# Deviations regrouped by two VectorE transposes and four small transfers instead of a TensorE product

## The chip, the cores and the metric

One core of one Trainium2 chip. The metric is the device time of one execution in microseconds; the median of several runs is quoted. Everything is float32. The engines of the core are TensorE (PE, with its weight loads PEld), VectorE (DVE), ScalarE (ACT), GpSimd (POOL) and SyncE (SP, which only issues transfers). Each runs its own instructions in order; semaphores hold one engine back for another, or for the landing of a transfer.

## The reference

Two blocks, one behind the other. The first mixes tokens by a filter in the frequency domain, the second is a feed-forward layer with a SoLU activation (h times its softmax) and a layer norm:

```python
batch, seq, dim = 8, 3136, 256            # 25088 tokens; d_ff = 1024
X = np.fft.rfft(x, axis=1)
Y = X * (filt_r + 1j * filt_i)[None]
t = np.fft.irfft(Y, n=3136, axis=1).reshape(25088, 256)

h = t @ w_in                               # 256 -> 1024
e = np.exp(h - h.max(-1, keepdims=True))
solu = h * e / (e.sum(-1, keepdims=True) + 1e-9)
mu = solu.mean(-1, keepdims=True)
var = ((solu - mu) ** 2).mean(-1, keepdims=True)
out = ((solu - mu) / np.sqrt(var + 1e-6) * g_ln) @ w_out   # 1024 -> 256
```

What the change touches is 1 / sqrt(var + ...), one number for each token ("deviation" in the code, `rs`). It scales the output rows of the last product.

## The kernel before

**Stages.** The first some 150 us convert the weights, transform batch element 0 and start element 1. From then on the feed-forward layer of the tokens that are ready runs together with the transforms of the later elements: element e's tokens are used while element e+1 is transformed. The last element's transform is over at about 1200 us; behind that only the feed-forward layer runs.

**Blocks, pairs, groups.** The 25088 tokens are 196 blocks of 128. Two blocks are a pair j (98 of them), because both products are done on pairs by a scheme with seven products of half size (`product(j, m)` at L759 and `project(p, m)` at L895, m = 1 to 7) and sums that GpSimd makes (`sum_of`, L738). Four blocks are a group g (49).

**Steps.** `step(k)` for k = 0 to 204 writes out by hand, for each engine, the order in which work of different blocks is interleaved: even and odd steps differ. A block passes `product`, `keep` (ScalarE copies a half of h from PSUM, L769), `finish` (VectorE makes another half and the row's maximum, L780 and L783), `exponential` (ScalarE, L793), `normalize` (VectorE, L805), `square` (ScalarE, the variance, L813), `turn` (VectorE transposes 32x32 blocks, L823), `regroup`, and some nine steps after its start `project`, `keep_out` (ScalarE, L911), `finish_out` (VectorE, L915) and `store_out` (SP, L923). No scheduler moves anything: each engine gets its instructions in the order in which the functions are called.

**Regrouping.** `project` needs solu with features on partitions. `turn` transposes only within 32x32 blocks, so `regroup` moves 32 partitions at a time by transfers from SP (L840, eight of 128 KB for a pair). The tokens then stand in another order: partition 32b + i of block a holds token 32a + i of block b of the group. The scale of an output row has to stand in the same order. That is what the changed part does, once for a group:

- `deviations(g)`, even step, GpSimd: variance plus floor (L850), power -1/2 (L851) into rs, 128 x 4 (partition: token in the block, column: block); then `wide` = rs times a table of zeros and ones, 128 x 4 x 32 (L853).
- `regroup_deviations(g)`, two steps later, behind `project(p, 4)`: one product on TensorE, `wide` as weights and four columns of the table (`turn_t`) as the moving side (L859, two passes), into four spare columns of a PSUM bank (`places`), and a copy by ScalarE into rs_t (L862).
- `keep_out` and `finish_out` take a column of rs_t as the scale.

**Queues.** SP issues the regroup transfers, the stores of the output, and in part of the steps the loads of x (L257); ScalarE and GpSimd issue the transforms' other loads and stores. All transfers that SP and ScalarE issue take eight completion semaphores in turn; a transfer is issued only when the last one on its semaphore has landed.

**PSUM.** `project(p, 2)` writes the bank that `finish_out(p - 1, 1, 0)` reads; `product(j, 4)` adds to a bank that `finish(j, k, 1)` reads. These are TensorE's two nearest waits for VectorE in an odd step.

Of the kernel before, what the change touches and what calls it, by code (L numbers as in the profile page):

```python
# [9 lines left out]
FP32 = mybir.dt.float32  # L10
I32 = mybir.dt.int32
AFT = mybir.ActivationFunctionType
ALU = mybir.AluOpType
# [4 lines left out]
P = 128  # L18
# [79 lines left out]
def kernel(  # L98
# [10 lines left out]
    nc = tc.nc  # L109
# [6 lines left out]
    there_dram = nc.inline_tensor(  # L116
        np.ascontiguousarray(de_host[:, :, 0].reshape(NP, P, P).transpose(1, 0, 2)), name="there_tbl").ap()
    one_dram = nc.inline_tensor(np.eye(P, dtype=np.float32), name="one_tbl").ap()
    rows = np.arange(P)[:, None]
    turn_dram = nc.inline_tensor(np.concatenate(  # L120
        [rows % 32 == np.arange(32), rows // 32 == np.arange(4)], 1).astype(np.float32),
        name="turn_tbl").ap()

    def pool(name, bufs, space=None, stack=ctx):
        kw = {} if space is None else {"space": space}
# [5 lines left out]
    small = pool("sm", 4)  # L131
# [15 lines left out]
    neg_half, floor_sb = small_consts[:, 0:4], small_consts[:, 4:5]  # L147
# [268 lines left out]
    with ExitStack() as st:  # L416
# [226 lines left out]
    def psum(name):  # L643
        return ps_t.tile([P, 2, C], FP32, name=name, tag="t")
# [13 lines left out]
             for name, bufs in (("r", 4), ("diff", 1), ("t2", 1), ("p", 1), ("g", 1))}  # L658
    pools["de"] = pool("de1", 2)
    spread = pool("spread", 1)  # L660
    turn_t = spread.tile([P, 36], FP32, name="turn_t", tag="turn_t")
    second.pools = pools
    for c, at, n, kind, dims in (
            (0, 0, 4 * C, "t2", "p (v c) -> p v c"), (0, 4 * C, 4 * C, "f", "p (v k c) -> p v k c"),
# [51 lines left out]
    def load_de(sp, u):  # L716
# [3 lines left out]
                            in_=de_dram[i:i + pairs].rearrange("i p k u q -> p i (k u q)"))  # L720
        return de

    turns, variances, solu_ts, solu_sums, spreads, rss, pos, ots, places, regrouped = (
        {} for _ in range(10))
    sums, ms, hs, nmaxs, es, esums, floors, solus, squares = ({} for _ in range(9))


# [120 lines left out]
    def deviations(g):  # L848
        rs = small.tile([P, 4], FP32, name=f"rs_{g}", tag="rs", bufs=2)
        nc.gpsimd.tensor_tensor(out=rs, in0=variances.pop(g), in1=floors.pop(g), op=ALU.add)  # L850
        nc.gpsimd.tensor_tensor(out=rs, in0=rs, in1=neg_half, op=ALU.pow)  # L851
        spreads[g] = wide = spread.tile([P, 4, 32], FP32, name=f"wide_{g}", tag="wide")
        nc.gpsimd.tensor_tensor(  # L853
            out=wide, in0=turn_t[:, 0:32].rearrange("p (o i) -> p o i", o=1).broadcast_to([P, 4, 32]),
            in1=rs.rearrange("p (b o) -> p b o", o=1).broadcast_to([P, 4, 32]), op=ALU.mult)

    def regroup_deviations(g, ps):

        nc.tensor.matmul(out=ps, lhsT=spreads.pop(g).rearrange("p b i -> p (b i)"), rhs=turn_t[:, 32:36],  # L859
                         start=True, stop=True)  # L860
        rss[g] = small.tile([P, 4], FP32, name=f"rs_t_{g}", tag="rs_t")
        nc.scalar.copy(out=rss[g], in_=ps)  # L862

    def project_sums(p, step):

# [14 lines left out]
    def project(p, m):  # L880

        alone = m == 3 and p in last
        bank = 2 if alone else {1: 0, 6: 0, 5: 0, 3: 0, 2: 1, 7: 1, 4: 1}[m]
        if alone:
            pos[p, bank] = ps_m.tile([P, DFF // 2], FP32, name=f"o{m}_{p}", tag="m0")[:, 0:P]
        elif m in (1, 2):
            ps = ps_o.tile([P, DFF // 2], FP32, name=f"o{m}_{p}", tag=f"o{bank}")
            pos[p, bank] = ps[:, 0:P]
            places[p] = ps[:, P:P + 4]
        s1, s2, s3, s4 = solu_sums[p]  # L890
        lhs = {1: solu_ts[p, 0][0], 2: solu_ts[p, 0][1], 4: solu_ts[p, 1][1], 5: s1, 6: s2, 7: s3,
               3: s4}[m]
        w = w_out_sb[:, {1: 0, 2: 1, 3: 2, 5: 3, 6: 4, 7: 5, 4: 6}[m]]
        for f in range(KF // 2):
            nc.tensor.matmul(out=pos[p, bank], lhsT=lhs[:, f, :], rhs=w[:, f, :],  # L895
                             start=f == 0 and (m in (1, 2, 7) or alone), stop=True,
                             skip_group_check=True)
# [104 lines left out]
    pairs = blocks // 2  # L1002

    def step(k):
        j, odd = divmod(k, 2)
        p = j - (LAG - 1) // 2 if odd else j - (LAG + 1) // 2
        if not 0 <= p < pairs:
            p = None
        hid, proj = k < blocks, p is not None
# [23 lines left out]
        if not odd:  # L1033
            if hid and k > LAG:
                product(j, 1)
                keep(j, k, 0)
            if 2 <= k < blocks:
                exponential(k - 2)
            if proj:
                project(p, 5)  # L1040
                keep_out(p, 1, (1, 1) if p in last else (0, 1))
            if p in last:
                keep_out(p, 0, (0, 1))
                finish_out(p, 1, 1, (1, 1), 1)
# [12 lines left out]
            if 3 <= k < blocks + 3:  # L1057
                square(k - 3)
            if hid:
                product(j, 6)  # L1060
                keep(j, k + 1, 0)
            if proj:
                project(p, 3)
                if p not in last:
                    keep_out(p, 0, (0, 1))
                project(p, 4)
            if j >= 4 and j % 2 == 0 and j - 4 < pairs:
                regroup_deviations((j - 4) // 2, places.pop(p) if proj else psum("ps_rs")[:, 0, 0:4])
            for job in spectrum_loads[k]:
                job()  # L1070
            if 0 <= j - 3 < pairs - 2:
                regroup(j - 3, 0)
                regroup(j - 3, 1)
            elif j - 3 == pairs - 2:
                regroup(j - 3, 1, nc.scalar.dma_start, range(2))
                regroup(j - 3, 0)
                regroup(j - 3, 1, parts=range(2, 4))
                regroup(j - 2, 0)
                regroup(j - 2, 1, parts=range(2))
            if 0 <= j - 4 < pairs:  # L1080
                project_sums(j - 4, 1)
            if j - 3 == pairs - 2:
                regroup(j - 2, 1, nc.gpsimd.dma_start, range(2, 4))
            if 0 <= j - 3 < pairs and j % 2:
                deviations((j - 3) // 2)
            if hid:
                product(j, 7)
            if p in last:
                finish_out(p, 0, 1, (0, 1), 2)
                finish_out(p, 1, 0, (1, 0), 1)  # L1090
                store_out(p)
            if 2 <= k < blocks + 2:
                normalize(k - 2)
            for job in second_parts[k] + middle[k] + first_parts[k]:
                job()
            if proj and p not in last:
                finish_out(p, 1, 0, (1, 0), 1)
                store_out(p)
        else:
            if hid and k >= LAG:  # L1100
                product(j, 5)
                keep(j, k - 1, 1)
                finish(j, k, 1, (k - 1, 1), 2)
            for job in early[k]:
                job()
            if proj:
                project(p, 1)
                keep_out(p, 0, (0, 0))
                project(p, 2)
                finish_out(p, 0, 0, (0, 0), 1)  # L1110
            if 2 <= k < blocks + 2:
                exponential(k - 2)
            if hid:
                product(j, 3)
                product(j, 4)
            if proj:
                project(p, 6)
                project(p, 7)
            for job in second_parts[k] + middle[k]:
                job()  # L1120
            if 3 <= k < blocks + 3:
                turn(k - 3)
            if hid:
                finish(j, k - 1, 1, None, 0)
                finish(j, k, 0, (k, 0), 2)
            if 2 <= k < blocks + 2:
                normalize(k - 2)
            if proj:
                keep_out(p, 1, (1, 0))
            if 3 <= k < blocks + 3:  # L1130
                square(k - 3)
            for job in first_parts[k]:
                job()
        if k == 0:
            for n in range(7):
                prepare_w_out(n)
# [2 lines left out]

    with tc.manual_schedule():  # L1140
        pair_sums(0)
        nc.gpsimd.dma_start(out=turn_t, in_=turn_dram)
        for load in first_loads:
            load()
        for k in range(blocks + LAG):
            step(k)
# [30 lines left out]
```

## Time and profile before

| | before |
|---|---|
| median of 3 runs | 1594.7 us (1591.9 to 1596.17) |
| the profiled execution: its time | 1601.33 us |
| its span, first to last instruction | 1599.6 us |
| mean granted TensorE clock | 0.994 |
| TensorE busy | 1551.8 us (97%) |
| VectorE busy | 1250.7 us (78%) |
| GpSimd busy | 1169.7 us (73%) |
| ScalarE busy | 921.4 us (58%) |
| bytes moved by DMA | 311.13 MB, mean 195 GB/s |

Busy time is that of instructions that work; register, semaphore and transfer-issuing instructions are not in it. Matmuls are pipelined, so the time from one start to the next, and not the duration of one, is what a matmul costs. SP has no work but to issue transfers; its entries carry a q, for its sequencer's queue.

### The profile page before, as it was taken

Reading aid. Unit: us, or ns where it says so; the run is one execution under the profiler, and the core shown is the slowest. Engines: PE = TensorE matmul, PEld = TensorE weight load, DVE = VectorE, ACT = ScalarE, POOL = GpSimd, SP = SyncE. Lnnn points to the kernel's source line nnn. Section 1 sums busy time; section 2 is a strip of 40 time slices with the busy share of each in tenths; the row PEclk is TensorE's granted clock in tenths of the full one; section 3 lists DMA queues with packets and bytes.
Section 4 is the critical chain, followed back from the end, with each engine's and each line's share of the span. In section 5 each row is a group of like instructions: output and inputs, shape, how many; then the busy total and the mean of one; then the engine's idle time right before and its main releaser. Section 6 shows DMA issues by size and latency. Waiting matters only on the chain.

```text
span 1599.6 us, 36769 instructions
## 1 busy us (share of the span) xinstructions
PE 1551.8 (97%) x12828; PEld 1058.8 (66%) x12828; DVE 1250.7 (78%) x2248; ACT 921.4 (58%) x1874; POOL 1169.7 (73%) x1371
## 2 busy tenths in 40 slices
PE   5998999999999999999999999999999999999997
PEld 1463566666666676677666677667766777777777
DVE  1887878897987788876988789887888777777673
ACT  2246555656665656666565655666565656666663
POOL 5546886789677868796779867797766766676765
PEclk8999999999999999999999999999999999999999
DMA  9989878786987589766886679766784444343434
GB/s 266 290 282 269 247 215 236 215 217 181 255 241 222 155 229 256 211 183 178 221 231 202 166 193 251 204 189 179 215 224 132 126 133 122 103 113 94 116 105 116
DMA packets 343802, 311.13 MB, mean 195 GB/s; under 512 B 27834, under 2 KB 310099, under 8 KB 343619
## 3 DMA queue, kind: packets, MB, share of 16 engines
q1 hardware_dynamic: 271476, 170.45, 40.6%
q0 software_dynamic: 33744, 98.81, 21.0%
q10 hardware_dynamic: 38400, 39.53, 8.2%
q8 instruction: 104, 1.70, 0.5%
q14 instruction: 78, 0.64, 0.1%
HBM read 124.51 MB, written 81.40 MB: 129 GB/s over the span
## 4 chain that ended last, share of the span: by engine, by line
PE 84%; DMA 9%; DVE 2%; POOL 1%; issue 1%; SPq 1%; ACT 0%; DVEq 0%; POOLq 0%; ACTq 0%
PE m L759 35%; PE o L895 34%; DMA solu_t<-turn 4%; PE py L386 4%; PE pc L313 3%; PE pb L313 3%; PE pa L281 2%; DMA x<-in_x_dram 2%; DMA f<-in_filt_r_dram 1%; SPq L840 1%; PE idler L563 1%; PE pa L238 1%; PE py L409 1%; DMA out_dram<-ot 1%; POOL u L738 1%
## 5 line engine op out<-in xcount | busy, mean ns | idle before, releaser
L895 PEld LDWEIGHTS o<-w_out_sb,solu_t 128*128 128x128 f32 x3136 | 381.5, 192 | 50.2 <-issue 43.6
L895 PE MATMUL o<-w_out_sb,solu_t 128*128 128x128 f32 x3136 | 400.9, 276 | 3.6 <-DVE ot L915 2.9
L759 PE MATMUL m<-w_in_sb,s 128*128 128x512 f32 x784 | 399.0, 610 | 2.7 <-ACT h L769 1.8
L895 PEld LDWEIGHTS o<-w_out_sb,u 128*128 128x128 f32 x2352 | 307.1, 192 | 138.9 <-issue 106.0
L895 PE MATMUL o<-w_out_sb,u 128*128 128x128 f32 x2352 | 310.6, 275 | 2.5 <-POOL u L738 1.8
L759 PE MATMUL m<-w_in_sb,y 128*128 128x512 f32 x588 | 307.6, 606 | 1.5 <-DVE h L780 1.1
L805 DVE SCALAR_TENSOR_TENSOR h<-e,h 128x1024 f32<-128x1024 f32 x196 | 304.1, 1551 | 0.1
L769 ACT COPY h<-m 128x512 f32<-128x512 f32 x294 | 173.2, 589 | 206.5 <-PE m L759 187.0
L911 ACT ACTIVATE ot<-o,rs_t 128x128 f32<-128x128 f32 x392 | 143.6, 368 | 245.2 <-PE o L895 243.8
L738 POOL TENSOR_TENSOR u<-solu_t 128x512 f32<-128x512 f32 x98 | 135.5, 1383 | 195.6 <-DMA solu_t<-turn 133.6
L783 DVE CUSTOM_DVE_ANT_0 h<-m,h 128x512 f32<-128x512 f32 x196 | 134.2, 685 | 176.8 <-ACT h L769 103.0
L813 ACT ACTIVATE h<-h,nmu 128x1024 f32<-128x1024 f32 x196 | 225.0, 1148 | 52.0 <-DVE turn L823 51.8
L823 DVE STREAM_TRANSPOSE turn<-h 128x1024 f32<-128x1024 f32 x196 | 243.1, 1240 | 3.2
L793 ACT ACTIVATE e<-h,nmax 128x1024 f32<-128x1024 f32 x196 | 225.4, 1150 | 7.9 <-DVE h L805 6.5
L738 POOL TENSOR_TENSOR u<-solu_t,u 128x512 f32<-128x512 f32 x98 | 137.7, 1405 | 95.8 <-PE o L895 95.5
L759 PEld LDWEIGHTS m<-w_in_sb,s 128*128 128x128 f32 x784 | 128.1, 191 | 89.5 <-issue 68.9
L915 DVE SCALAR_TENSOR_TENSOR ot<-o,rs_t,ot 128x128 f32<-128x128 f32 x299 | 103.7, 347 | 98.8 <-ACT ot L911 59.0
L738 POOL TENSOR_TENSOR u<-u,solu_t 128x512 f32<-128x512 f32 x98 | 159.1, 1624 | 15.5 <-PE o L895 6.4
L759 PEld LDWEIGHTS m<-w_in_sb,y 128*128 128x128 f32 x588 | 96.6, 191 | 96.7 <-issue 46.6
L738 POOL TENSOR_TENSOR solu_t<-solu_t,solu_t 128x512 f32<-128x512 f32 x98 | 153.9, 1571 | 0.9
L738 POOL TENSOR_TENSOR s<-y 128x128 f32<-128x128 f32 x196 | 99.8, 509 | 0.5
L386 PEld LDWEIGHTS py<-wb_t,t 50*64 50x64 f32 x3584 | 57.6, 134 | 42.9 <-issue 18.7
(126 smaller groups left out, 1969.1 us busy)
## 6 DMA issues: line engine op xcount, KB each, us to landing
solu_t<-turn SPq DMA_DIRECT2D x780, 128.0 KB
out_dram<-ot SPq DMA_DIRECT2D x196, 128.0 KB
t<-d POOLq DMA_DIRECT2D x112, 200.0 KB, 7.0
d<-x POOLq DMA_DIRECT2D x100, 200.0 KB, 5.3
f<-f_dram POOLq DMA_DIRECT2D x39, 512.0 KB, 8.1
t<-d ACTq DMA_DIRECT2D x37, 512.0 KB
d<-g POOLq DMA_DIRECT2D x36, 512.0 KB, 5.1
x<-in_x_dram SPq DMA_DIRECT2D x112, 98.0 KB
```

The costliest lines, as they stand in the source:

```text
L386: nc.tensor.matmul(out=views[g][64 * h:64 * h + 64, cb, i, :], lhsT=t4[rows, i, c0:c0 + 64], rhs=wb_t[rows, 0:N1], start=True, stop=True)
L738: nc.gpsimd.tensor_tensor(out=out, in0=in0, in1=in1, op=op)
L759: nc.tensor.matmul(out=ms[j, bank], lhsT=lhsT, rhs=w_in_sb[:, w, :], start=m in (1, 2, 7), stop=True, skip_group_check=True)
L769: nc.scalar.copy(out=h_half(k, i), in_=ms[j, 0])
L783: nc.vector.tensor_tensor_reduce(out=h_half(k, i), in0=ms[j, bank], in1=h_half(*kept), scale=1.0, scalar=sofar, op0=ALU.add, op1=ALU.min, ...
L793: nc.scalar.activation(out=e, in_=hs[k], func=AFT.Exp, bias=nmaxs.pop(k)[:, 1:2], scale=-1.0, accum_out=esums[g][:, i:i + 1])
L805: nc.vector.scalar_tensor_tensor(out=solu, in0=e, scalar=SHRINK, in1=solu, op0=ALU.mult, op1=ALU.mult, accum_out=nmu)
L813: nc.scalar.activation(out=solu, in_=solu, func=AFT.Square, bias=nmu, scale=-float(DFF), accum_out=variances[g][:, i:i + 1])
L823: nc.vector.transpose(out=turns[g][:, :, i, :], in_=solus[k].rearrange("p (f j) -> p f j", j=32))
L895: nc.tensor.matmul(out=pos[p, bank], lhsT=lhs[:, f, :], rhs=w[:, f, :], start=f == 0 and (m in (1, 2, 7) or alone), stop=True, skip_group_ ...
L911: nc.scalar.activation(out=out_half(p, *to)[0], in_=pos[p, 0], func=AFT.Copy, scale=rs)
L915: nc.vector.scalar_tensor_tensor(out=ot, in0=pos[p, bank], scalar=rs, in1=out_half(p, *kept)[0], op0=ALU.mult, op1=ALU.add)
```

## The change

`deviations` ends with the power -1/2, which is written into the first four columns of a cleared tile `lines` (128 x 32). A new function, called at the end of the odd step that follows, transposes `lines` on VectorE by 32x32 blocks and has SP move four times four rows of 32 numbers (512 bytes a transfer) to the partitions where a second transpose can pick them up. `regroup_deviations`, at its old place in the step, is now that second transpose, into an rs_t of 128 x 32 of which four columns are used. The table, `wide`, the product on TensorE, its place in PSUM and the copy by ScalarE are gone.

```diff
@@ pools
-    turn_t = spread.tile([P, 36], FP32, name="turn_t", tag="turn_t")
+    lines = small.tile([P, 32], FP32, name="lines", tag="lines", bufs=1)
+    turned_rs, crossed_rs = (spread.tile([P, 32], FP32, name=n, tag=n) for n in ("turned_rs", "crossed_rs"))
+    for cleared in (lines, crossed_rs):
+        nc.gpsimd.memset(cleared, 0.0)
@@ def deviations(g):
         nc.gpsimd.tensor_tensor(out=rs, in0=variances.pop(g), in1=floors.pop(g), op=ALU.add)
-        nc.gpsimd.tensor_tensor(out=rs, in0=rs, in1=neg_half, op=ALU.pow)
-        spreads[g] = wide = spread.tile([P, 4, 32], FP32, name=f"wide_{g}", tag="wide")
-        nc.gpsimd.tensor_tensor(
-            out=wide, in0=turn_t[:, 0:32].rearrange("p (o i) -> p o i", o=1).broadcast_to([P, 4, 32]),
-            in1=rs.rearrange("p (b o) -> p b o", o=1).broadcast_to([P, 4, 32]), op=ALU.mult)
-
-    def regroup_deviations(g, ps):
-
-        nc.tensor.matmul(out=ps, lhsT=spreads.pop(g).rearrange("p b i -> p (b i)"), rhs=turn_t[:, 32:36],
-                         start=True, stop=True)
-        rss[g] = small.tile([P, 4], FP32, name=f"rs_t_{g}", tag="rs_t")
-        nc.scalar.copy(out=rss[g], in_=ps)
+        nc.gpsimd.tensor_tensor(out=lines[:, 0:4], in0=rs, in1=neg_half, op=ALU.pow)
+
+    def cross_deviations(g):
+
+        nc.vector.transpose(out=turned_rs, in_=lines)
+        to = crossed_rs.rearrange("(b r) i -> r b i", r=32)
+        for a in range(4):
+            nc.sync.dma_start(out=to[a], in_=turned_rs[32 * a:32 * a + 4])
+
+    def regroup_deviations(g):
+        rss[g] = spread.tile([P, 32], FP32, name=f"rs_t_{g}", tag="rs_t", bufs=4)
+        nc.vector.transpose(out=rss[g], in_=crossed_rs)
@@ def step(k), even steps
             if j >= 4 and j % 2 == 0 and j - 4 < pairs:
-                regroup_deviations((j - 4) // 2, places.pop(p) if proj else psum("ps_rs")[:, 0, 0:4])
+                regroup_deviations((j - 4) // 2)
@@ def step(k), end of odd steps
             for job in first_parts[k]:
                 job()
+            if 0 <= j - 3 < pairs and j % 2:
+                cross_deviations((j - 3) // 2)
```

Also gone are the table in DRAM and its load (`nc.gpsimd.dma_start(out=turn_t, in_=turn_dram)`), and `places`.

More of the change, by code (lines that the diff above doesn't have):

```diff
@@ L118 @@
     one_dram = nc.inline_tensor(np.eye(P, dtype=np.float32), name="one_tbl").ap()
[L119 to L122, printed above, removed]
     def pool(name, bufs, space=None, stack=ctx):
@@ L721, in load_de @@
         return de
-    turns, variances, solu_ts, solu_sums, spreads, rss, pos, ots, places, regrouped = (
-        {} for _ in range(10))
+    turns, variances, solu_ts, solu_sums, rss, pos, ots, regrouped = (
+        {} for _ in range(8))
     sums, ms, hs, nmaxs, es, esums, floors, solus, squares = ({} for _ in range(9))
@@ L888, in project @@
             pos[p, bank] = ps[:, 0:P]
-            places[p] = ps[:, P:P + 4]
         s1, s2, s3, s4 = solu_sums[p]
@@ L1141 @@
         pair_sums(0)
-        nc.gpsimd.dma_start(out=turn_t, in_=turn_dram)
         for load in first_loads:
```

## The prediction

> **What bounds the kernel now.** I read the page first, then the busy time by stretch, the groups, SP's own waits, and last the timelines of one place where the change sits.
>
> ```profile
> span 1599.6 us, 36769 instructions
> PE 1551.8 (97%) x12828; PEld 1058.8 (66%) x12828; DVE 1250.7 (78%) x2248; ACT 921.4 (58%) x1874; POOL 1169.7 (73%) x1371
> PE 84%; DMA 9%; DVE 2%; POOL 1%; issue 1%; SPq 1%; ACT 0%; DVEq 0%; POOLq 0%; ACTq 0%
> ```
>
> TensorE is the bound: busy 97% of the span and 84% of the chain that ended last. So TensorE time taken away is gained in full, and every wait put in front of TensorE is lost in full. The stretches tell how much room the others have:
>
> ```profile
> 600.00:800.00 200.00, 199.99 (x1867) 138.59 (x1866) 165.09 (x299) 121.16 (x249) 157.53 (x187) 1.00 0.77 210
> 1400.00:1500.00 100.00, 100.00 (x578) 72.67 (x577) 73.82 (x139) 63.08 (x131) 70.74 (x77) 1.00 0.40 106
> ```
>
> The columns are busy us of TensorE, its weight loads, VectorE, ScalarE and GpSimd, then the clock and the DMA share. Until about 1200 us VectorE is busy 83% and the DMA engines 77%; after it 74% and 40%. TensorE leaves nothing unused in either.
>
> **What is removed.** Groups by form, with the mean ns of one after the busy time:
>
> ```profile
> L859 PE MATMUL o<-turn_t,wide 128*128 128x4 f32 x96 | 13.6, 212 | 0.0
> L862 ACT COPY rs_t<-o 128x4 f32<-128x4 f32 x48 | 7.8, 162 | 25.4 <-PE o L859 25.4
> L823 DVE STREAM_TRANSPOSE turn<-h 128x1024 f32<-128x1024 f32 x196 | 243.1, 1240 | 3.2
> ```
>
> Matmuls overlap, so 212 ns is not what one costs TensorE. In the timeline the first pass of L859 starts at 805.26 and the product behind it at 805.40. In every even step with L859 the last pass of project 4 is followed by product 7 after 0.254 us, in every one without it after 0.112 us. So one regrouping costs TensorE 0.142 us, and 49 cost 7.0 us. That is the gain. The 49 copies on ScalarE (8 us, and 25.4 us of waiting for L859) and the 49 multiplications on GpSimd (49 x 0.40 = 20 us) lie beside TensorE; I price them at nothing, because ScalarE is idle 42% and GpSimd 27%. Two clears of small tiles and one table load at the start change sides, beside the first 120 us.
>
> **What is added on VectorE.** 98 transposes of 128x32. The only transpose in the trace takes 1.240 us for 1024 columns; 32 of them would be 0.04 us, and the shortest VectorE row is 0.08 us. Between 0.04 and 0.35 (L915, 128x128) I take 0.1 us: 10 us of VectorE in all, small beside its idle 349 us. It enters below as 0.1 us on each side of the transfers.
>
> **What is added on SP, and the new wait.** In the order of the built program the first transpose of a group stands at the end of an odd step, behind normalize (L805). The four transfers follow in SP's queue, ahead of the next eight regroup transfers (L840). The second transpose stands in the middle of the next even step, right in front of the next L805, and waits for all four landings. VectorE runs in order, so L805, the spectrum's products, the joins, finish_out (L915) and the next step's finish (L783) queue behind that wait. Group 20 in the trace of before, VectorE:
>
> ```profile
> 799.31 0.08 DVE L805 DVE_READ_ACCUMULATOR h<-e,h 128x1 f32 x1
> 799.42 1.25 DVE L823 STREAM_TRANSPOSE turn<-h 128x1024 f32<-128x1024 f32 x1
> 800.72 0.69 DVE L783 CUSTOM_DVE_ANT_0 h<-m,h 128x512 f32<-128x512 f32 x1
> 802.05 0.35 DVE L915 SCALAR_TENSOR_TENSOR ot<-o,rs_t,ot 128x128 f32<-128x128 f32 x1 [0.63 <-ACT ot L911]
> 802.32 2.13 DVE L805 SCALAR_TENSOR_TENSOR h<-e,h 128x1024 f32<-128x1024 f32 x1
> ```
>
> The first transpose would start at 799.39, the second is due at 802.32: a window of 2.9 us. Over the groups it is 2.05 to 4.3 us (one 7.8). SP's timeline there, and two rows of its waits:
>
> ```profile
> 798.02 14.07 SPq L840 DMA_DIRECT2D solu_t<-turn  x8
> 799.68 1.79 SPq L840 DMA_DIRECT2D solu_t<-turn  x1
> 805.39 0.58 SPq L840 DMA_DIRECT2D solu_t<-turn  x1
> ```
>
> ```profile
> SPq L840 <- DMA out_dram<-ot: 46.6, 41, 3.9
> SPq L840 <- DMA solu_t<-turn: 19.6, 20, 2.5
> ```
>
> The transfers of SP and ScalarE use eight semaphores in turn, and each waits until the last holder of its semaphore has landed. The fourth regroup transfer here could only go at 805.39, because its semaphore belonged to a store of the output that SP issued at 793.68. In the changed order the four small transfers take exactly these places in the queue and in the turn. So the fourth goes at 805.4, not at 801.
>
> Price of one trip. Issue: L257 and L840 take 0.29 to 0.75 us on SP where they don't wait, with no order by size; I take 0.45, with 0.15 and 0.65 as ends. From the end of the issue to the landing: a regroup transfer between partitions on an empty queue takes 1.71 to 1.76 us (the fastest tenth), the quickest store 2.8 us; I take 1.74, since the new transfers also stay in SBUF. Another 0.2 us before and after for transpose and semaphore. With nothing in the way: 0.2 + 4 x 0.45 + 1.74 + 0.2 = 3.9 us, 1 us over the usual window. In group 20: 805.4 + 0.45 + 1.74 + 0.2 = 807.8, a VectorE stall of 5.5 us.
>
> The Trainium skill ("DMA: Bandwidth & Descriptors", section "Anatomy of one DMA — SWDGE (gpsimd) path") gives about 2.0 us as the fixed cost of any transfer, on a path other than SP's. By that figure the loss below would be 60 us and not 55.
>
> What the stall costs TensorE:
>
> ```profile
> 807.28 0.34 DVE L915 SCALAR_TENSOR_TENSOR ot<-o,rs_t,ot 128x128 f32<-128x128 f32 x1
> 807.20 1.95 PE L895 MATMUL o<-w_out_sb,solu_t 128*128 128x128 f32 x16
> ```
>
> The second eight of these 16 passes (project 2, from 808.09) write the bank that L915 frees at 807.62. The slack is 0.5 us, so TensorE would lose 5.0 us here. I read window, semaphore landings and slack (the smaller of project 2 behind L915 and product 4 behind L783, plus VectorE's idle time between) the same way at groups 0 to 47:
> - 21 groups before 1200 us with loads of x (L257) just ahead in SP's queue: stalls of 69.6 us, of which slack leaves 47.4.
> - 13 other groups of that stretch: 16.3 us of stall, 7.6 left.
> - 14 groups after it: 16.8 us of stall, slack 1.5 to 3.0 us, nothing left.
> - The last group: its transfers stand behind two output stores that SP issues at 1580.74 and 1581.44, so the second transpose ends near 1586 where the L915 behind it ran at 1578.43. TensorE then waits in project 2 of pair 96 from 1579.6, less what it waits there anyway for GpSimd until 1582.5: 5 us.
>
> Loss 55 + 5, gain 7: +53 us on the profiled execution of 1601.3 us, 3.3%. On the median of 1594.7 us that is 1647 us. The ends: with 0.15 us an issue the 55 is 44, with 0.65 it is 64, with stores' landings of 2.8 us 75; so +42 to +73, 1637 to 1668. Given back by less crowded queues at a slower pace: 0 to 20 us, taken as nothing.
>
> The regroup transfers behind the four: in loaded groups the first four go up to 8 us later, the other four (due at 6 to 8 us after the first transpose) 2 to 3 us later. GpSimd waits 133.6 us for them already (44 times) and TensorE waits behind these sums hardly at all, some 13 us; so I price this at nothing. If that cover fails, 2 us in each of 34 groups is 68 us.
>
> The Trainium skill ("VectorE: DVE Perf Modes", section "Rules for kernel authors") sends a 128x128 transpose to TensorE where PSUM will do, since VectorE's covers 32x32 blocks only. Here the row speaks on the same side from its price: 0.142 us of TensorE against a trip of 3.9 us.
>
> **The rivals.**
> 1. Forecast, 0.60: the trip outlasts the slack in the loaded groups; 1647, own range 1620 to 1675.
> 2. Faster, 0.17: the trip fits into window and slack everywhere. Its place is the 21 loaded groups; it decides where four transfers land within 3.9 us of the first transpose, that is, if the semaphores ahead are free in time. For it: windows plus slack are 4.7 to 6.1 us after 1200 us. Against it: SP's fourth regroup issue, 4 to 9 us after the first transpose's place in 12 of those groups. Then only the 7.0 us count: 1588.
> 3. No change, 0.07: loss and gain cancel, with 7 us of stall left over from the 55; 1590 to 1599.
> 4. Worse, 0.16: slack does not come back between groups, or regrouping becomes late. VectorE has 5 us idle in a group of 29 us, less than the stall of a loaded group; with all 104 us of stall before 1200 us at the dear issue counted, +102 us: 1697; with the 68 us of late regrouping 1715.
> That the change does not do what it says is out: the built order has 98 transposes, 196 such transfers and no L859.
>
> **How the numbers follow.** A measurement of this kernel tells about 0.3% from no change. Faster 0.17, same 0.07, slower 0.76. The range leaves out the lower half of case 2 and most of case 4 above 1690: 1588 to 1690.
>
> **What would show it.** Right: VectorE's wait in front of the second transpose is a large new row, released by the small transfers, some 85 us before 1200 us and 17 us after; TensorE's new idle time ends on L915; the stretch 1400 to 1500 does as much work as before. Wrong: a mean trip under 3 us; TensorE idle where no second transpose precedes; or GpSimd's wait for regrouped tokens grown and TensorE waiting behind it.

## The result, and the profile after

| | before | after |
|---|---|---|
| median of 6 runs each, same chip | 1595.4 us | 1652.2 us |
| ratio, 95% interval | | 1.0354 [1.0321, 1.0388] |
| the profiled execution: its time, its span | 1601.3, 1599.6 us | 1664.4, 1662.3 us |
| mean granted TensorE clock | 0.994 | 0.979 |

The changed kernel is 3.5% slower, some 57 us. Its profiled execution is the slowest of its six runs, so differences between the two traces (62.7 us of span) are a little larger than that between the medians.

The head of the page of the changed kernel:

```profile
span 1662.3 us, 36908 instructions
PE 1563.2 (94%) x12730; PEld 1062.2 (64%) x12730; DVE 1248.9 (75%) x2346; ACT 914.7 (55%) x1825; POOL 1145.6 (69%) x1323
```

98 passes fewer on TensorE, 98 instructions more on VectorE. TensorE's idle time has gone from 47.8 us (1599.6 - 1551.8) to 99.1 us, and its busy time has gone up by 11.4 us although it has less to do. Both need an answer. The stretches of the changed kernel, with columns as in the prediction:

```profile
600.00:800.00 200.00, 193.52 (x1745) 133.33 (x1745) 158.35 (x301) 116.29 (x235) 147.46 (x175) 0.99 0.74 202
1400.00:1500.00 100.00, 100.00 (x687) 72.40 (x687) 75.59 (x148) 62.34 (x125) 71.27 (x72) 1.00 0.40 106
```

While the transforms run, TensorE loses 6.5 us in 200; behind them it loses nothing. The waits, with engine, line, what is waited for, then us in total, times and the longest. First two rows of before, then those of the changed kernel, then SP's own wait in it:

```profile
POOL u L738 <- DMA solu_t<-turn: 133.6, 44, 8.2
PE o L895 <- DVE ot L915: 2.9, 4, 1.2
```

```profile
DVE rs_t L861 <- DMA crossed_rs<-turned_rs: 116.4, 48, 8.9
POOL u L737 <- DMA solu_t<-turn: 122.9, 42, 8.7
PE o L893 <- DVE ot L913: 52.5, 26, 7.6
```

```profile
SPq L857 <- DVE turned_rs L854: 163.2, 41, 7.6
```

The row of L861 is new: in 48 of 49 groups VectorE stands in front of the second transpose until the small transfers land. The row of L893 is the price: TensorE waits 52.5 us for `finish_out` (now L913), for which the trace of before has 2.9 us in 4 waits. GpSimd's wait for regrouped tokens (122.9 us, 133.6 before) has not grown.

One group shows the chain from VectorE's wait to TensorE's. Group 20, VectorE in the changed kernel:

```profile
832.29 0.20 DVE L854 STREAM_TRANSPOSE turned_rs<-lines 128x32 f32<-128x32 f32 x1
...
835.37 0.35 DVE L913 SCALAR_TENSOR_TENSOR ot<-o,rs_t,ot 128x128 f32<-128x128 f32 x1
838.89 0.21 DVE L861 STREAM_TRANSPOSE rs_t<-crossed_rs 128x32 f32<-128x32 f32 x1 [3.17 <-DMA crossed_rs<-turned_rs]
839.02 2.03 DVE L804 SCALAR_TENSOR_TENSOR h<-e,h 128x1024 f32<-128x1024 f32 x1
```

SP and TensorE at the same place:

```profile
832.52 2.87 SPq L857 DMA_DIRECT2D crossed_rs<-turned_rs  x4
835.60 8.78 SPq L839 DMA_DIRECT2D solu_t<-turn  x8
```

```profile
841.01 1.05 PE L893 MATMUL o<-w_out_sb,solu_t 128*128 128x128 f32 x8
844.25 1.61 PE L893 MATMUL o<-w_out_sb,solu_t 128*128 128x128 f32 x8 [2.19 <-DVE ot L913]
```

The first transpose ends at 832.49, SP needs until 835.39 for the four issues, and the last landing comes after 838.8. VectorE has had nothing to do since 835.7 and stands 3.17 us. Then L804 (2 us), the joins and L913 follow late, and TensorE stands 2.19 us in front of the second eight passes of L893: the place that the prediction named.

The busy time that grew has another cause. Right behind that stall the stretches read (same columns):

```profile
842.00:844.30 2.30, 0.11 (x2) 0.05 (x1) 2.27 (x6) 1.49 (x3) 0.00 (x0) 1.00 0.73 198
844.50:847.50 3.00, 3.00 (x11) 1.97 (x11) 2.43 (x6) 0.00 (x0) 2.54 (x5) 0.55 1.07 285
848.50:852.00 3.50, 3.50 (x41) 2.65 (x39) 3.50 (x7) 1.99 (x5) 0.73 (x1) 1.00 0.41 112
```

TensorE is idle, then busy at a granted clock of 0.55, then at 1.00 again. The trace's clock records give it the half clock from 844.8 to 848.2. There are 4 such stretches in the trace of before (19.8 us together) and 17 in that of after (72.3 us). Those of after are 3.4 or 6.8 us long except the one at the very end, and nearly each stands beside a stall of TensorE. If half the time is lost at half clock, that is an estimate of (72.3 - 19.8) / 2 = 26 us that do not show as idle.

The end of the program answers to the prediction's last item. VectorE, TensorE and SP in the last group:

```profile
1642.27 0.21 DVE L861 STREAM_TRANSPOSE rs_t<-crossed_rs 128x32 f32<-128x32 f32 x1 [8.92 <-DMA crossed_rs<-turned_rs]
```

```profile
1643.03 2.08 PE L893 MATMUL o<-w_out_sb,solu_t 128*128 128x128 f32 x8 [7.57 <-DVE ot L913]
```

```profile
1636.64 1.30 SPq L921 DMA_DIRECT2D out_dram<-ot  x2
1638.03 2.28 SPq L857 DMA_DIRECT2D crossed_rs<-turned_rs  x4
```

The four transfers stand behind two stores; the wait is 7.57 us.

### The profile page after: what moved, and what is told of

Its sections match the earlier page's. It is cut to its first block, busy times and chain, and to the rows that moved or that the text cites. A ratio compares the mean times of both kernels' runs of the same rounds, so it can differ in the third digit from the quotient of the medians.

```text
span 1662.3 us, 36908 instructions
## 1 busy us (share of the span) xinstructions
PE 1563.2 (94%) x12730; PEld 1062.2 (64%) x12730; DVE 1248.9 (75%) x2346; ACT 914.7 (55%) x1825; POOL 1145.6 (69%) x1323
## 5 line engine op out<-in xcount | busy, mean ns | idle before, releaser
L893 PE MATMUL o<-w_out_sb,solu_t 128*128 128x128 f32 x3136 | 412.5, 279 | 52.7 <-DVE ot L913 52.5
L893 PEld LDWEIGHTS o<-w_out_sb,solu_t 128*128 128x128 f32 x3136 | 389.1, 195 | 102.1 <-DVE ot L913 58.0
L758 PE MATMUL m<-w_in_sb,s 128*128 128x512 f32 x784 | 404.2, 618 | 3.2 <-ACT h L768 1.4
L893 PEld LDWEIGHTS o<-w_out_sb,u 128*128 128x128 f32 x2352 | 310.4, 193 | 140.8 <-issue 110.3
L758 PE MATMUL m<-w_in_sb,y 128*128 128x512 f32 x588 | 313.1, 616 | 5.9 <-DVE nmax L782 3.8
L804 DVE SCALAR_TENSOR_TENSOR h<-e,h 128x1024 f32<-128x1024 f32 x196 | 315.8, 1611 | 0.3 <-issue 0.2
L893 PE MATMUL o<-w_out_sb,u 128*128 128x128 f32 x2352 | 312.5, 277 | 1.4 <-ACT ot L909 1.4
L737 POOL TENSOR_TENSOR u<-solu_t 128x512 f32<-128x512 f32 x98 | 133.8, 1365 | 190.2 <-DMA solu_t<-turn 122.9
L782 DVE CUSTOM_DVE_ANT_0 h<-m,h 128x512 f32<-128x512 f32 x196 | 134.1, 684 | 148.4 <-ACT h L768 74.7
L737 POOL TENSOR_TENSOR u<-solu_t,u 128x512 f32<-128x512 f32 x98 | 141.1, 1440 | 109.5 <-PE o L893 109.2
L913 DVE SCALAR_TENSOR_TENSOR ot<-o,rs_t,ot 128x128 f32<-128x128 f32 x299 | 103.2, 346 | 75.6 <-ACT ot L909 47.1
L737 POOL TENSOR_TENSOR solu_t<-solu_t,solu_t 128x512 f32<-128x512 f32 x98 | 145.3, 1482 | 0.9
L268 POOL TENSOR_TENSOR x<-x 113x512 f32<-113x512 f32 x48 | 61.1, 1272 | 67.1 <-DVE diff L262 66.8
L737 POOL TENSOR_TENSOR s<-y 128x128 f32<-128x128 f32 x196 | 105.1, 536 | 0.7 <-DMA y<-in_x_dram 0.3
```

The lines of the kernel that those rows point to most:

```text
L268: nc.gpsimd.tensor_tensor(out=xi[rows, 0:2, :], in0=xi[rows, 0:2, :], in1=xi[rows, 2:4, :], op=ALU.add)
L737: nc.gpsimd.tensor_tensor(out=out, in0=in0, in1=in1, op=op)
L758: nc.tensor.matmul(out=ms[j, bank], lhsT=lhsT, rhs=w_in_sb[:, w, :], start=m in (1, 2, 7), stop=True, skip_group_check=True)
L782: nc.vector.tensor_tensor_reduce(out=h_half(k, i), in0=ms[j, bank], in1=h_half(*kept), scale=1.0, scalar=sofar, op0=ALU.add, op1=ALU.min, ...
L804: nc.vector.scalar_tensor_tensor(out=solu, in0=e, scalar=SHRINK, in1=solu, op0=ALU.mult, op1=ALU.mult, accum_out=nmu)
L913: nc.vector.scalar_tensor_tensor(out=ot, in0=pos[p, bank], scalar=rs, in1=out_half(p, *kept)[0], op0=ALU.mult, op1=ALU.add)
```

## The experiments

Three theories stood against each other. The **wait** theory is the prediction's: the second transpose stands too early on VectorE, and what is queued behind it comes late. The **hold** theory: the four transfers wait in SP's queue for the first transpose, and what stands behind them there (the regroup transfers, the loads of x) comes late. The **own cost** theory: four more transfers per group, each with a place in the turn of the eight semaphores, cost something wherever they stand. The expectations of the first four experiments call the wait theory just "theory" and the other two together "rival"; the later ones call the own cost "turn theory" (for the turn of the semaphores) or "load theory"; "queue theory" is hold and turn together. A ratio r is turned into us as (r - 1) x 1597, and every ratio is to the kernel before on the same chip. "T1" and "T2" are the first and the second transpose.

**The second transpose later.** Edit to the changed kernel: T2 stands behind `finish_out(p, 1, 0)` and `store_out(p)`, the last place in the even step from which its readers are served in time.

```diff
@@ even step
-            if j >= 4 and j % 2 == 0 and j - 4 < pairs:
-                regroup_deviations((j - 4) // 2)
...
                 store_out(p)
+            if j >= 4 and j % 2 == 0 and j - 4 < pairs:
+                regroup_deviations((j - 4) // 2)
```

> The changed kernel with the second transpose moved from in front of normalize to the end of the same even step, behind finish_out and store_out; nothing else differs. Theory (the wait in front of normalize is what costs): the trips measured in the changed kernel, 3.3 to 9.4 us, fit into the window there in all but five groups, and slack covers those, so TensorE's wait for L913 goes from 52.5 us to under 8 us, the granted clock is back at 0.99, and the 7 us of TensorE work stay saved; the last group's transfers still stand behind two stores, +4 us. 1592 us, between 1587 and 1598. Rival (the four transfers hold up the regroup transfers behind them on SP and in the turn of semaphores): nothing is gained, over 1630 us.

Measured: 1.0161 [1.0124, 1.0198], +26 us. Its waits:

```profile
DVE rs_t L861 <- DMA crossed_rs<-turned_rs: 34.3, 14, 7.4
PE o L893 <- DVE ot L913: 3.6, 7, 0.8
PE m L758 <- DVE nmax L782: 11.8, 8, 4.1
```

TensorE's wait for L913 is back from 52.5 to 3.6 us, and over half of the loss with it. So the wait is the larger part. But 26 us remain, where the saved product alone would give a gain: taking the wait away did not bring back the time before. The median, 1624.9 us, lies in neither forecast.

**No transfers.** Edit to the changed kernel: the four issues and the tile `crossed_rs` are gone, and T2 reads `turned_rs`, so the scales stay on the wrong partitions.

```diff
-        to = crossed_rs.rearrange("(b r) i -> r b i", r=32)
-        for a in range(4):
-            nc.sync.dma_start(out=to[a], in_=turned_rs[32 * a:32 * a + 4])
...
-        nc.vector.transpose(out=rss[g], in_=crossed_rs)
+        nc.vector.transpose(out=rss[g], in_=turned_rs)
```

> The changed kernel without the four transfers: the second transpose reads what the first one wrote, so the scales stay on the wrong partitions; the movement between partitions is left out. Both theories: no trip and nothing on SP, so what is left is the gain, 49 x 0.142 = 7 us of TensorE, against 98 transposes of 0.2 us on VectorE. Theory: these 20 us lie in VectorE's idle time, 1588 us, between 1584 and 1592. A third theory (the transposes themselves load VectorE where it has no idle time): above 1600.

Measured: 0.9940 [0.9918, 0.9962], a gain of 10 us; the median, 1586.5 us, is as forecast. TensorE's row of the page and its wait for `finish_out`:

```profile
PE 1536.2 (97%) x12730; PEld 1045.8 (66%) x12730; DVE 1254.9 (79%) x2346; ACT 913.4 (58%) x1825; POOL 1146.8 (72%) x1322
```

```profile
PE o L890 <- DVE ot L910: 1.3, 4, 0.4
```

With the same TensorE instructions the changed kernel has 27.0 us more busy time (1563.2 against 1536.2) and 52.1 us more idle time (99.1 against 47.0). Everything that was lost comes from the transfers and the waits that they bring; 98 transposes and the lighter TensorE, ScalarE and GpSimd are a gain. The 27 us of busy time fit the 26 us estimated for the clock.

**The transfers added to the kernel before.** T1 and the four transfers as in the changed kernel, the product on TensorE kept; the transfers carry zeros, and nobody reads `crossed_rs`.

```diff
+    lines = small.tile([P, 32], FP32, name="lines", tag="lines", bufs=1)
+    turned_rs, crossed_rs = (spread.tile([P, 32], FP32, name=n, tag=n) for n in ("turned_rs", "crossed_rs"))
...
+    def cross_deviations(g):
+        nc.vector.transpose(out=turned_rs, in_=lines)
+        to = crossed_rs.rearrange("(b r) i -> r b i", r=32)
+        for a in range(4):
+            nc.sync.dma_start(out=to[a], in_=turned_rs[32 * a:32 * a + 4])
@@ end of odd steps
+            if 0 <= j - 3 < pairs and j % 2:
+                cross_deviations((j - 3) // 2)
```

> The kernel before, its product on TensorE kept, with the first transpose and the four transfers added at the places that they have in the changed kernel (they carry zeros that nobody reads), and no second transpose. Theory: nobody waits for them, and the cover of the regroup transfers holds: 1595 us, at most 1600, TensorE's wait for L915 at the 3 us of before. Rival (late regroup transfers): 1630 us or more, with TensorE or GpSimd waiting longer for solu_t.

Measured: 1.0276 [1.0247, 1.0305], +44 us, without any wait of VectorE for them: the rival's range, not the theory's. That is much more than what stayed in the first experiment, so this sum does not come out yet.

**The same with the wait.** The kernel of the third experiment and a transpose of `crossed_rs` at T2's place, whose result nobody reads.

```diff
+                nc.vector.transpose(out=again, in_=crossed_rs)
```

> As the kernel before with transfers, and the second transpose added in front of normalize as in the changed kernel (its output is not used; the product on TensorE is kept). Theory: the wait alone brings the whole loss, and the 7 us are not saved: 1595 + 57 + 7 = 1659 us, between 1648 and 1670, TensorE's wait for L915 about 50 us and the clock near 0.98. Rival: within 10 us of the kernel with the transfers alone.

Measured: 1.0552 [1.0521, 1.0583], +88 us, or 44 us more than without the wait. The median, 1684.3 us, is above the theory's range, which gave the transfers no cost of their own, and far from the rival's. Its waits:

```profile
DVE again L1080 <- DMA crossed_rs<-turned_rs: 123.2, 48, 10.9
PE o L906 <- DVE ot L926: 55.4, 20, 8.8
```

The wait of the changed kernel is reproduced to a few us (116.4 and 52.5 there), by a transpose that does nothing else. That is the wait theory shown from the other side: 44 us.

**Another queue.** The third kernel with the transfers issued by GpSimd, and then the first with them issued by GpSimd. The edit in both:

```diff
-            nc.sync.dma_start(out=to[a], in_=turned_rs[32 * a:32 * a + 4])
+            nc.gpsimd.dma_start(out=to[a], in_=turned_rs[32 * a:32 * a + 4])
```

> The kernel before with the first transpose and the four transfers added (nobody reads them), as in the run that lost 43 us, but GpSimd issues the transfers instead of SP. What is open: adding transfers that nobody waits for on VectorE cost 43 us, against our 0. Queue theory (SP stands still until the first transpose has run, and x loads and regroup transfers behind go late; the four also take half a round of the eight semaphores): with GpSimd none of that happens, 1597 to 1606 us. Load theory (four more transfers on the DMA engines, or the added tiles and the transpose, cost by themselves): still over 1630 us.

> The kernel with the late second transpose, its transfers issued by GpSimd instead of SP. Queue theory: neither the wait in front of normalize nor SP's queue is left, the 7 to 10 us of TensorE stay saved, the last group's transfers no longer stand behind two stores: 1590 us, between 1584 and 1600. Load theory: as with SP, 1616 to 1632 us.

Measured: 1.0251 [1.0203, 1.0298] and 1.0144 [1.0103, 1.0185], +40 and +23 us, against +44 and +26 from SP. GpSimd's wait for T1 in the first, then in the second of them:

```profile
POOL crossed_rs L872 <- DVE turned_rs L869: 136.6, 41, 5.6
```

```profile
POOL crossed_rs L857 <- DVE turned_rs L854: 155.4, 42, 6.2
```

SP's queue is clear in both, and GpSimd's transfers take no part in the eight semaphores. But GpSimd computes, and now stands for T1 itself. The two runs exchange one wait for another, so they do not separate the theories; they show that the other queue is no way out (1639.5 and 1622.5 us, both in the load theory's range).

**Transfers that wait for nothing.** The third kernel without T1: the transfers copy `lines`, which was cleared at the start and is not written again.

```diff
-        nc.vector.transpose(out=turned_rs, in_=lines)
...
-            nc.sync.dma_start(out=to[a], in_=turned_rs[32 * a:32 * a + 4])
+            nc.sync.dma_start(out=to[a], in_=lines[32 * a:32 * a + 4])
```

> As the kernel before with the four transfers on SP, but without the first transpose: they copy a tile that was cleared at the start, so SP issues them as soon as it reaches them and their semaphores are free. Hold theory (SP's wait for the first transpose, 123 us in 34 waits, is what delays the loads behind it): 1596 to 1606 us. Turn theory (four issues of 0.6 us and four more holders in the turn of the eight semaphores, for which SP and ScalarE wait): 1625 to 1645 us, as before.

Measured: 1.0248 [1.0196, 1.0300], +40 us against +44 held. The hold theory wanted most of the loss to go with the hold, and it stayed: 1637.7 us, in the range of the turn theory.

**T1 earlier and T2 later.** The first experiment's kernel, with `cross_deviations` in front of the odd step's `turn` instead of at the end of the step.

```diff
@@ odd step
+            if 0 <= j - 3 < pairs and j % 2:
+                cross_deviations((j - 3) // 2)
             # (turn of the step stands here)
...
-            if 0 <= j - 3 < pairs and j % 2:
-                cross_deviations((j - 3) // 2)
```

> The kernel with the late second transpose (1624.9 us), and now the first transpose and its four transfers earlier too: in front of turn in the same odd step, some 4 us sooner on VectorE. Hold theory: SP waits for the first transpose much shorter (137 us before, under 60 us now), 1598 to 1612 us. Turn theory: nothing in the turn changes, 1616 to 1632 us.

Measured: 1.0078 [1.0055, 1.0101], +12 us, the best version without the product that computes everything. Its waits:

```profile
DVE rs_t L861 <- DMA crossed_rs<-turned_rs: 31.1, 13, 7.8
PE o L893 <- DVE ot L913: 2.4, 4, 1.0
PE m L758 <- DVE nmax L782: 13.3, 12, 2.0
```

VectorE's row is like that of the first experiment (31.1 against 34.3), and yet it is 13 us faster, with intervals that do not overlap. The two programs differ in T1's place on VectorE alone; SP's instructions are the same, in the same order. What has gone is SP's wait for T1, in the first experiment and here:

```profile
SPq L857 <- DVE turned_rs L854: 137.2, 35, 6.7
```

```profile
SPq L857 <- DVE turned_rs L854: 15.0, 8, 4.1
```

The median, 1609.4 us, is in the range of the hold theory and below that of the turn theory. So with a late T2 the hold is worth some 13 us; by which waits they reach TensorE was not followed. The kernel is still slower than before, although TensorE does less.

**Only a tile more.** What did the third kernel add besides transfers? In the built programs the new tile `lines`, 128 bytes a partition, stands in the pool `small`, and every tile allocated behind that pool (solu_t, x, turn and others) begins 128 bytes later: solu_t at 145024 instead of 144896, which is a multiple of 512. The kernel of the third experiment has that shift, and so have the three made from it above (with the wait, with GpSimd's queue, without T1). The changed kernel has not, because it also moves rs_t out of `small`. So: before, with a tile of that size which nobody uses.

```diff
+    unused = small.tile([P, 32], FP32, name="unused", tag="unused", bufs=1)
+    nc.gpsimd.memset(unused, 0.0)
```

> The kernel before with one unused cleared tile of 128 bytes a partition in the pool of small tiles, and nothing else. Open: three kernels that keep the product and add transfers lost 40 to 43 us, whoever issued them and whether or not they were held. In all of these the added tile moves every later tile by 128 bytes: the regrouped tokens and x then start 128 bytes past a multiple of 512, where in the kernel before, the changed kernel and those with a late second transpose they start on a multiple of 512. Shift theory: the regroup transfers write pieces of 512 bytes, and off their boundary they take longer: 1628 to 1641 us with the tile alone. Otherwise 1598 us.

Measured: 1.0110 [1.0071, 1.0148], +18 us, by a shift of addresses and one clear at the start. The median, 1615.8 us, lies between the two forecasts: the shift costs something, but less than its theory said. Waits for x, before and with the tile:

```profile
DVE diff L266 <- DMA x<-in_x_dram: 12.6, 9, 2.8
```

```profile
DVE diff L266 <- DMA x<-in_x_dram: 19.7, 12, 3.2
```

**The transfers without the shift.** The third kernel and the one without T1, with `lines` in the last pool, so that every other tile is where it was before.

```diff
-    lines = small.tile([P, 32], FP32, name="lines", tag="lines", bufs=1)
+    lines = spread.tile([P, 32], FP32, name="lines", tag="lines")
```

> The kernel before with the first transpose and the four transfers on SP, nobody reading them, as in the run that lost 43 us, but with the added tile in the last pool, so that no other tile moves. Shift theory alone: 1598 to 1604 us. Hold theory beside it (SP stands still until the first transpose has run): from the late second transpose against no transfers at all, both on their boundary, 36 us: 1618 to 1636 us.

> The same, no tile moved, without the first transpose: the four transfers copy a constant tile and SP issues them when it reaches them. Hold theory: 1598 to 1606 us. Turn theory (the four issues and their places in the turn of eight semaphores cost by themselves): within 8 us of the kernel with the held transfers.

Measured: 1.0122 [1.0087, 1.0157] held for T1 and 1.0102 [1.0074, 1.0129] not held, +19 and +16 us. The first (1616.9 us) is above the range of the shift alone and just under that of the hold theory; the second (1613.3 us) is above the hold theory's range and within 8 us of the first, as the turn theory said. Waits of the held one, then of the other:

```profile
POOL u L742 <- DMA solu_t<-turn: 187.2, 51, 8.7
DVE diff L266 <- DMA x<-in_x_dram: 31.2, 18, 5.3
```

```profile
POOL u L742 <- DMA solu_t<-turn: 155.6, 53, 9.1
DVE diff L266 <- DMA x<-in_x_dram: 19.0, 12, 4.1
```

Now the sums nearly come out: 18 us shift and 19 us transfers make 37 of the third kernel's 44 [39, 49], and 18 and 16 make 34 of the 40 [31, 48] without T1. The four transfers cost 16 to 19 us by themselves, with no one waiting for them. The hold is worth 3 us between these two, and the intervals overlap. GpSimd's wait differs by more (187.2 against 155.6 us, 133.6 before), but it is no measure of the cost: it is 155.6 us in the run without transfers too, which is 10 us faster than before:

```profile
POOL u L737 <- DMA solu_t<-turn: 155.6, 53, 7.8
```

**The transfers between the regroup transfers.** The kernel with T1 earlier and T2 later, with the four issues taken out of `cross_deviations` and placed between the first and the second four regroup transfers of the next even step, when T1 is long done.

```diff
+                if j >= 4 and j % 2 == 0:
+                    send_deviations()
```

> A version made from what was found: first transpose in front of turn, second at the end of the even step, tiles on their boundary, and SP issues the four transfers between the first four and the last four regroup transfers of the even step, where it waits for TensorE anyway, so that it stands still for the first transpose nowhere. Hold theory: the hold is gone and 7 to 10 us of TensorE stay saved but for the last group's 5: 1590 to 1600 us against 1609 with the transfers in their old place. Turn theory: as there, 1604 to 1614 us.

Measured: 1.0223 [1.0176, 1.0270], +36 us (1635.2 us), 23 us worse than without it and above both forecasts. Its waits:

```profile
DVE rs_t L863 <- DMA crossed_rs<-turned_rs: 71.4, 20, 10.2
PE m L758 <- DVE nmax L782: 32.3, 14, 7.7
```

No hold of SP for T1 is left (1.9 us), but the small transfers queue behind four of 128 KB, T2 waits twice as long as in the kernel it comes from, and TensorE waits 32.3 us instead of 13.3 for `finish` (L782), which stands behind T2 on VectorE. One wait was taken away and another lengthened, so this run does not judge the hold theory; it shows that this place is a worse one.

**The account**, in us of 1597: leaving out the product and its helpers -10 (no transfers), four transfers in SP's queue and in the turn +19 (held, aligned), and the rest of +57, put down to the wait of T2: 47. The wait measured for itself was 44 (88 - 44). With T2 late the rest is 16 instead of 47, and with T1 early as well about 3 (12 + 10 - 19). These two rests are not T2's wait alone: from the one to the other VectorE's wait hardly changes (34.3 and 31.1 us), and SP's wait for T1 goes. The parts need not add exactly, but three kernels that were not used to get them agree to within 7 us: transfers with shift 37 against 44, without T1 34 against 40, and transfers, shift and wait 84 against 88.

So the hold costs 13 us in one pair of kernels and 3 us, not clear of noise, in another. Why the two differ is open.

What stays open is where the 16 to 19 us of the transfers' own cost arise. In these kernels TensorE's new idle time is spread over many small waits (for x, for sums of regrouped tokens, for the maximum), and no single row carries it. That four more holders in the turn of eight semaphores delay what comes behind them fits, since 16 us are left where nothing is held; but no run changed the number of semaphores, so it was not shown. How a shift of 128 bytes costs 18 us is open as well: in that trace a regroup transfer lands in the median 4.68 us after the end of its issue instead of 4.45, between 200 and 1150 us, but on an empty queue as fast as before (1.71 to 1.74 us). No kernel with other shifts was run.

## Why the prediction was right

The forecast, that the trip outlasts the slack in the loaded groups, held in total (3.5% against 3.3%) and in place. By its steps:

- **The gain of 7.0 us.** Without the transfers the changed kernel gains 10 us [6, 13]. Right, and what was priced at nothing (copies, multiplications, 98 transposes) is nothing or a small gain.
- **The transposes.** The two rows of the changed kernel:

```profile
L854 DVE STREAM_TRANSPOSE turned_rs<-lines x49: 198/200/211, 169.4 to 1632.9; 128x32 f32<-128x32 f32 x49
L861 DVE STREAM_TRANSPOSE rs_t<-crossed_rs x49: 211/211/214, 176.1 to 1642.3; 128x32 f32<-128x32 f32 x49
```

  The numbers behind the colon are the shortest, median and longest duration in ns. 0.2 us each, twice the estimate; it changes nothing.
- **One trip.** 3.9 us were forecast for an empty queue; the quickest took 3.3 us from the end of T1 to the last landing. Two terms were off, in opposite directions: issues follow one another at 0.62 us and not 0.45 (within the ends named), and on an empty queue the small transfer lands 1.0 us after the end of its issue and not 1.74. A row of 128 KB was too dear for 512 bytes. The Trainium skill's 2.0 us ("DMA: Bandwidth & Descriptors", section "Anatomy of one DMA — SWDGE (gpsimd) path") is further off; it is stated for another path than SP's and covers setup as well as completion. From the start of the issue the quickest landing took 1.5 us here, and the measurement decides.
- **The stalls.** VectorE waits 90.7 us in groups 0 to 33, 19.6 in groups 34 to 47 and 8.9 in the last; the prediction said 85.9 (69.6 + 16.3), 16.8 and some 8. The trip was a median of 4.3 us and up to 9.35 us. The sums agree better than their parts. In group 20 the prediction had the fourth transfer held by its semaphore until 6.0 us after T1's place, and a stall of 5.5 us; it was issued 2.4 us after T1, landed 3.5 us after the end of its issue and not 1.74, and the stall was 3.17 us. Over groups 0 to 33 the fourth issue came a median of 1.85 us after T1 and over 4 us after it in four groups, where the prediction counted 12 groups with 4 to 9 us; and the small transfers landed a median of 2.2 us after the end of their issue, against 1.0 us in groups 34 to 47. A term that was too large and one that was too small met, and that is luck.
- **Slack.** The same model of windows and slack, with the measured trips, gives 46.5 us for groups 1 to 47; TensorE's waits for L913 are 52.5 us with the last group's 7.57. Predicted 55 + 5. Once the transforms are over, slack takes nearly everything: the changed kernel even gains about 0.4 us in every 4 pairs there, near the 0.28 us of two saved products. Two readings of the prediction miss a group: its slack of 1.5 to 3.0 us after 1200 us leaves out group 47 with 0.06 us, where TensorE now waits 1.92 us, and its one long window of 7.8 us leaves out group 0 with 7.1 us.
- **The clock: a term that was missing.** 26 us on this execution. TensorE's stalls were counted at their length, but a stall can be followed by 3.4 us or more at half clock. Between 138 and 1231 us the changed kernel has 14 such stretches, each beside a stall; 12 of these stalls last 2.1 to 3.3 us, the other two 3.8 and 4.4. One more stall of 2.2 us was not followed by half clock, nor were the four of 1.0 to 1.7 us there. The Trainium skill ("TensorE: Matmul & The Clock Gate", section "HAM oscillation — how this bites in real kernels") states as its abstract rule that idle gaps above some 3.4 us are to be avoided. By that rule only 2 of the 14 would be expected, so here the measurement says that 2 us can be enough, if not each time.
- **Regrouping behind the four: priced at nothing.** The sign that the prediction named for this did not show: GpSimd's wait in the changed kernel did not grow. But the transfers do cost 16 to 19 us where nobody waits for them, and the account has that cost in the changed kernel too, since the wait adds 44 us on top of it. GpSimd's wait was the wrong place to look: from the third experiment to the fourth, which adds only the wait of T2, it falls from 190.1 to 119.0 us while the kernel gets 44 us slower. The prediction asked what the transfers cost the queue only beside the stall, and not in the best version of the change, where with T1 early and T2 late that cost outweighs the gain: 16 to 19 less 10 is 6 to 9 of the 12 us.

So the mechanism and its place were right, and the total was right partly by luck. On the medians of the experiments the wait is worth 44 to 47 us, its half clock included, where the prediction had 60 without any; the transfers' own cost is 16 to 19 us, where it had nothing; the gain is 10 us, where it had 7. The sum is 57 us against 53. On the traces, single executions of which the changed kernel's was the slowest of its six (1664.4 us), the transfers brought 52 us of idle and 27 us of busy time, and the kernel without them is 16 us shorter than before (1599.6 - 1583.2): 63 us against 53. On the medians the forecast, 1647 us, is 5 us too low.

The rivals: VectorE waits in 48 of 49 groups and TensorE 26 times for L913, so the trip does not fit into window and slack, and the faster case is out. Slack does come back between groups: of the 119 us that VectorE waits, 52.5 reach TensorE, and the late regroup transfers cost far less than the 68 us named, so the worse case is out too.

## What to carry to other kernels

On an engine that runs in order, the place of a waiting instruction costs more than the instruction: two transposes of 0.2 us cost 44 to 47 us because the second waits in front of work that TensorE needs. Beside the gain and the transfers' own cost, 16 us of that were left with the second transpose at the end of the step, and about 3 with the first one earlier as well. Price a stall of TensorE with the half clock behind it, and price a transfer by its place in the queue even if no one waits for it: replacing 0.142 us of the busiest engine by a trip over partitions lost in each of the five versions that made the trip. When a tile is added for an experiment, keep the addresses of the others, or measure the tile alone.

## What the runs showed of the hardware that was not expected

- A stall of TensorE of 2.1 to 3.3 us can be followed by 3.4 us (sometimes 6.8) at a granted clock of half: in all 72.3 us of the changed kernel against 19.8 us before.
- 128 bytes more in front of the large tiles, with no work added but one clear, cost 1.1% [0.7, 1.5].
- A transfer of 512 bytes between partitions landed 1.0 us after the end of its issue on an empty queue, one of 128 KB 1.7 us; SP issued the small ones every 0.62 us. Beside the transforms' traffic the small ones took a median of 2.2 us.
- A transpose of 128x32 takes 0.20 us and one of 128x1024 1.24 us, so a small one is far from a 32nd of the large one.
- 196 small transfers that nobody waits for cost 1.0 to 1.2% of this kernel.
